# An FFT convolution with a gated GLU, forward and backward: four offset streams, two-bank PSUM tiles, and crossbar transposes moved into the GLU stage

## The chip, the core and the metric

One core of a Trainium2 chip runs the whole program. Its engines work side by side: PE (TensorE) multiplies matrices and writes only to PSUM; DVE (VectorE) and ACT (ScalarE) do elementwise work and carry PSUM to SBUF; POOL (GpSimd) and SP (SyncE) here mostly issue DMAs. The DMAs of all queues run on 16 DMA engines. The metric is the device time of one execution in microseconds, lower is better, as the median of several runs. A profile is one further execution, recorded by the hardware.

## The reference

The function has two halves that share a layer-normalized input, and the kernel returns its value and nine gradients:

```
def _A_ref(q, k, v, shift_k, ssm_k, ssm_D):       # S = 2048, D = 512, L = 2S
    k_shift = sum over t<4 of k_pad[:, t:t+S] * shift_k[:, 3-t]
    kv = k_shift * v
    y = irfft(rfft(kv_pad) * rfft(kf_pad))[:S]     # long convolution over S, per channel
    y = y + kv * ssm_D
    return q * y
def _B_ref(x, w_gate, w_up, w_down):               # F = 1376
    h = sigmoid(x @ w_gate) * (x @ w_up)
    return h @ w_down
xn = layernorm(A_q)
out = A_q + _A_ref(xn, A_k, A_v, ...) * silu(_B_ref(xn, ...))
# returned: out and the gradients of q, k, v, shift_k, ssm_k, ssm_D, w_gate, w_up, w_down for grad_out
```

All inputs and outputs are bf16.

## The kernel before, in words

Tokens lie so that token 16p + j is at partition p of block j: 16 blocks (NJ) of 128 tokens. The 512 channels are worked in four groups (NG) of 128 (GW). The 4096-point transform is a product of matrix steps on PE: `step1` multiplies by a cosine and sine table (Cf), `flip` transposes on PE, `step3` applies a small block-diagonal table (BD), `cmul` is the complex product on DVE (L411 to L415, four instructions), and `inv3`, `inv1` go back with R and Ci, the transposed table. Between steps each PSUM tile is carried to SBUF by `bal.evac` (L114), which gives the copy to ACT (it then shows as L121) or DVE (L124), whichever has the smaller sum of estimated work so far.

SBUF is one slab, from which an allocator hands out rings; a ring's tile can be written again when its last user is done. PSUM is one pool of eight banks of 2 KB: four one-bank tiles "mm", two "acc", two "tr".

The work is written as generators that yield after a piece of PE work. `run_streams` always advances the one with the smallest share of its total done, so the program's text order mixes them. The compiler of the kernel then orders each engine's instructions by that priority and by a timing model of its own, and sets the waits; on the chip each engine and each DMA queue runs its list in order.

Stage A (L545 to L549): `gluA` does the first LAG = 4 token blocks of the GLU's forward half (`f_gen`), `frontA` transposes ssm_k, forms k_shift and kv (`shift`: eight DVE instructions of 2048 elements in a row), and does step1 for both; `backA` does the rest and leaves y in y2A, and both spectra in the DRAM scratch KK_d.

Stage B (`stepB`, L677): 88 PE transposes of w_gate and w_up (`wT_prep`), then for each token block i: `z_gen` (h @ w_down, the gate, the output o0, dz), `d_gen` (dh, then dg and du), `f_gen(i+4)`, and `x_gen` (the gradient of x through the layer norm, o1). f_gen computes psG, its sigmoid on ACT, psU, and the product h on DVE. h, dg and du are feature-major (features on partitions); they are stored to the DRAM scratch hT_d, dgT_d, duT_d by the POOL queue.

Stage C (L886 to L890): `dW` forms the three weight gradients in nine jobs. Each job needs a token-major block L of h, dg or du of 2 MB; `ld_L` loads it with four crossbar transposes from DRAM on the SP queue (L743), two jobs ahead. `frontC` and `backC` do the backward FFT group by group: step1 on dy, flips, step3, two complex products with the spectra loaded by `ld_KK` (SP queue, L792), inverse steps, then the gradients of v, k, shift_k, ssm_k. A one-token shift inside SBUF (L842, 127 partitions) feeds the gradients of k and shift_k. Outputs go out on the POOL queue; dW's pass through a ring of three tiles (ot).

Of the kernel before, what the change touches and what calls it, by code (L numbers as in the profile page):

```python
# [8 lines left out]
ACT = mybir.ActivationFunctionType  # L9
# [20 lines left out]
LAG = 4  # L30
SLAB = 206 * 1024
# [95 lines left out]
def run_streams(streams, until=None):  # L127

    live = [[g, 0.0, float(tot)] for g, tot in streams]
    while live:  # L130
        if until is not None and until():
            return [(g, t - d) for g, d, t in live]
        order = sorted(live, key=lambda s: s[1] / s[2])
        for s in order:
            try:
                c = next(s[0])
            except StopIteration:
                live.remove(s)
                break
            if c:  # L140
                s[1] += c
                break
        else:
            raise RuntimeError("all streams blocked")
    return []
# [8 lines left out]
def gen_fft_consts(nc, ar, negpi, Cf, BD, R):  # L154
# [4 lines left out]
    def tmp(shape, dt):  # L159
# [8 lines left out]
    nc.vector.tensor_tensor(m, a[:, :, None].to_broadcast([P, 16, 128]),  # L168
                            b[:, None, :].to_broadcast([P, 16, 128]), ALU.mult)
    mc = tmp([2, 16, 128], i32)  # L170
    nc.vector.tensor_single_scalar(mc[:, 0], m, 6144, ALU.add)
    nc.vector.tensor_single_scalar(mc[:, 0], mc[:, 0], 8191, ALU.bitwise_and)
    nc.vector.tensor_single_scalar(mc[:, 1], m, 8191, ALU.bitwise_and)
    mf = tmp([2, 16, 128], f32)
    nc.vector.tensor_copy(mf, mc)
    nc.scalar.activation(Cf, mf, ACT.Sin, bias=negpi, scale=sc)
# [40 lines left out]
def kernel_impl(ctx, tc, A_q, A_k, A_v, A_shift_k, A_ssm_k, A_ssm_D, B_x, B_w_gate, B_w_up, B_w_down,  # L217
# [9 lines left out]
    hT_d = dram.tile([NJ * P, FP], bf16, name="hT_d")  # L227
    dgT_d = dram.tile([NJ * P, FP], bf16, name="dgT_d")
    duT_d = dram.tile([NJ * P, FP], bf16, name="duT_d")
# [4 lines left out]
    psp = ctx.enter_context(tc.tile_pool(name="ps", bufs=1, space=PSUM))  # L234
    bal = Bal(nc)

    def ps_mm(shape, dt=f32, name="ps_mm"):
        return psp.tile([P] + shape, dt, name=name, tag="mm", bufs=4)

    def ps_acc(shape, dt=f32, name="ps_acc"):  # L240
        return psp.tile([P] + shape, dt, name=name, tag="acc", bufs=2)

    def ps_tr(shape, dt=bf16, name="ps_tr"):
        return psp.tile([P] + shape, dt, name=name, tag="tr", bufs=2)

# [19 lines left out]

# [6 lines left out]
    make_identity(nc, ident)  # L272
    nc.vector.memset(neghalf, -0.5)
    T = [dict() for _ in range(NJ)]

# [17 lines left out]
    def f_gen(i):  # L293
# [4 lines left out]
        bal.evac(xnT, pt[:], 512, half=True)  # L298
# [5 lines left out]
        for pi, (f0, nb) in enumerate(FBS):  # L304
            psG = ps_mm([4, 128], name="psG")
            for b in range(nb):
                for db in range(4):
                    nc.tensor.matmul(psG[:, b, :], wg[:, db, (f0 + b) * 128:(f0 + b + 1) * 128], xnT[:, db, :],  # L308
                                     start=(db == 0), stop=(db == 3))
            nc.scalar.activation(sigT[:, f0:f0 + nb, :], psG[:, 0:nb, :], ACT.Sigmoid)  # L310
            bal.act(nb * 128)
            yield nb * 512
            psU = ps_mm([4, 128], name="psU")
            for b in range(nb):
                for db in range(4):
                    nc.tensor.matmul(psU[:, b, :], wu[:, db, (f0 + b) * 128:(f0 + b + 1) * 128], xnT[:, db, :],  # L316
                                     start=(db == 0), stop=(db == 3))
            nc.vector.tensor_tensor(hT[:, f0:f0 + nb, :], psU[:, 0:nb, :], sigT[:, f0:f0 + nb, :], ALU.mult)  # L318
# [3 lines left out]
            yield nb * 512  # L322
        nc.gpsimd.dma_start(hT_d[i * P:(i + 1) * P, :], hT.rearrange("p a t -> p (a t)"))


    f_x(0)
    f_x(1)
    nc.scalar.dma_start(wg[:, :, 0:F], B_w_gate.rearrange("(db p) f -> p db f", p=P))
    nc.sync.dma_start(wu[:, :, 0:F], B_w_up.rearrange("(db p) f -> p db f", p=P))
    nc.gpsimd.memset(wg[:, :, F:FP], 0.0)  # L330
    nc.gpsimd.memset(wu[:, :, F:FP], 0.0)
    with nc.allow_non_contiguous_dma(reason="tiny"):
        nc.gpsimd.dma_start(Dcol_b, A_ssm_D.rearrange("(cg p) -> p cg", p=P))
    f_ln(0)
    skr_r = Ring(ar, [D * 4])
    ones_r = Ring(ar, [P])
    skr, ones1 = skr_r.ap[0:1, :], ones_r.ap[0:1, :]
    nc.gpsimd.dma_start(skr, A_shift_k.rearrange("(o d) t -> o (d t)", o=1))
    nc.vector.memset(ones1, 1.0)
    gen_fft_consts(nc, ar, negpi, Cf, BD, R)  # L340
# [8 lines left out]
    Ci_r = Ring(ar, [2, 16, 128])  # L349
    Ci = Ci_r.ap  # L350
    KT_r = Ring(ar, [S])
    KC_r = Ring(ar, [NJ, GW])
    kh_r = Ring(ar, [NJ + 3, 2 * GW])
    vg_r = Ring(ar, [NJ, 2 * GW])
    acc_r = Ring(ar, [NJ, GW])
    term_r = Ring(ar, [NJ, GW])
    kvt_r = Ring(ar, [NJ, GW])
    QgK_r = Ring(ar, [2, GG, NJ, 8])
    QgV_r = Ring(ar, [2, GG, NJ, 8])
    Qf_r = Ring(ar, [2, GG, 128], n=1)  # L360
# [6 lines left out]
    flags = set()  # L367
    stA = {}

    def gen_ci():  # L370
        for c in range(2):
            for jh in range(2):
# [3 lines left out]
                bal.evac(Ci[:, c, 8 * jh:8 * jh + 8, :], pt[:], 1024, half=True)  # L376
                yield 1024

    def step1(src, Qg):
        for jb in range(4):  # L380
            for c in range(2):
                ps = ps_mm([4, GW], name="ps_q")
                for jj in range(4):
                    j = jb * 4 + jj
# [566 lines left out]
```

## Time and profile before

| what | value |
|---|---|
| runs of the kernel | 747.41, 748.88, 762.13 us; median 748.88 |
| profiled execution, its own time | 755.69 us |
| its span, first to last instruction | 753.9 us |
| mean granted TensorE clock | 0.919 |
| busy: PE, DVE, ACT, POOL | 586.7, 443.5, 371.6, 146.0 us |
| DMA | 94.83 MB in 113545 packets, 79926 of them under 512 B |
| stage A, to the first psZ matmul of stage B | 215.6 us |
| stage B, to the last psX matmul | 235.5 us |
| stage C | 302.8 us |

Busy time is the time in which an engine executes; its share of the span averages stages with different limits, so the stages are read apart. A row such as "L411 DVE TENSOR_TENSOR slab<-slab 128x1024 bf16 x48 | 33.1, 690 | 134.5 <-ACT slab L121 132.1" gives line, engine, operation, tiles and count; the busy time and the mean of one in ns; then the engine's idle time just before these instructions, and what ended it. "PEld" is the loading of weights into PE. The granted clock is the share of full speed that PE had. DMA share is the mean busy share of the 16 DMA engines.

### The profile page before, as it was taken

How to read it: one execution, taken by the hardware profiler on the slowest of the kernel's cores; microseconds unless marked ns; L12 is line 12 of the kernel's file. 1: busy time of each engine (PE TensorE's matmuls, PEld its weight loads, DVE VectorE, ACT ScalarE, POOL GpSimd, SP SyncE). 2: the span in 40 equal slices, each digit the busy share in tenths (PEclk: the TensorE clock that was granted, in tenths of full speed). 3: DMA queues.
4: the chain of work that ended last, by engine and by line, in shares of the span. 5: the costliest groups of instructions: out<-in, count | busy, mean ns of one | idle time of the engine just before them, and what ended most of it. 6: DMA issues, size and time to landing. Idle time of an engine off the chain costs nothing. (4 is left out here: it accounts for less than half of the span.)

```text
span 753.9 us, 13216 instructions
## 1 busy us (share of the span) xinstructions
PE 586.7 (78%) x5340; PEld 386.3 (51%) x5340; DVE 443.5 (59%) x904; ACT 371.6 (49%) x588; POOL 146.0 (19%) x224
## 2 busy tenths in 40 slices
PE   2277386788879999999999789599949944996650
PEld 1265174656647767776775444256425622554430
DVE  4399469583857877887787661027607520662643
ACT  3475285778744334433442222177517801782770
POOL 4012121120201111111111133000510230015011
PEclk9998598899999999999999899799979986998985
DMA  5425423134422232323229279669766699635106
GB/s 178 144 87 173 148 80 123 64 112 102 167 78 99 94 145 86 108 95 143 87 98 220 94 159 215 114 133 235 200 107 157 179 160 81 148 124 142 67 23 67
DMA packets 113545, 94.83 MB, mean 126 GB/s; under 512 B 79926, under 2 KB 97036, under 8 KB 113484
## 3 DMA queue, kind: packets, MB, share of 16 engines
q1 hardware_dynamic: 97580, 43.29, 26.5%
q0 software_dynamic: 15376, 49.30, 22.2%
q10 hardware_dynamic: 528, 1.41, 0.5%
q8 instruction: 41, 0.67, 0.4%
q14 instruction: 20, 0.16, 0.1%
HBM read 32.28 MB, written 42.51 MB: 99 GB/s over the span
## 5 line engine op out<-in xcount | busy, mean ns | idle before, releaser
L411 DVE TENSOR_TENSOR slab<-slab 128x1024 bf16<-128x1024 bf16 x48 | 33.1, 690 | 134.5 <-ACT slab L121 132.1
L772 PE MATMUL psW<-slab 128*128 128x512 bf16 (+1 forms) x384 | 86.2, 370 | 30.9 <-ACT slab L121 30.9
L427 PE MATMUL ps_b<-slab 128*128 128x256 bf16 x384 | 63.0, 298 | 34.7 <-DVE slab L414 33.8
L658 PE MATMUL psX<-slab 128*128 128x512 bf16 x352 | 82.5, 390 | 0.4 <-DVE slab L643 0.3
L121 ACT CAST slab<-ps_b 128x512 bf16<-128x512 f32 x96 | 52.4, 592 | 53.3 <-PE ps_b L427 51.7
L772 PEld LDWEIGHTS <-slab 128*128 128x128 bf16 x384 | 37.4, 99 | 64.9 <-issue 34.4
L427 PEld LDWEIGHTS <-slab 128*128 128x128 bf16 x384 | 33.9, 104 | 67.4 <-DVE slab L414 54.7
L121 ACT CAST slab<-ps_q 128x512 bf16<-128x512 f32 x82 | 47.2, 616 | 43.1 <-PE ps_q L385 30.8
L121 ACT CAST slab<-psW 128x512 bf16<-128x512 f32 (+1 forms) x35 | 20.0, 575 | 83.3 <-DMA out_dram<-slab 61.0
L658 PEld LDWEIGHTS <-slab 128*128 128x128 bf16 x352 | 34.2, 100 | 41.5 <-issue 2.9
L755 PE MATMUL psW<-slab 128*128 128x512 bf16 x176 | 44.0, 397 | 9.6 <-ACT slab L121 9.6
L308 PE MATMUL psG<-slab 128*128 128x128 bf16 x704 | 49.1, 224 | 0.6 <-DVE slab L318 0.4
L316 PE MATMUL psU<-slab 128*128 128x128 bf16 x704 | 48.8, 223 | 0.3
L639 PE MATMUL psD<-slab 128*128 128x128 bf16 x704 | 46.6, 220 | 1.2 <-ACT slab L121 1.2
L308 PEld LDWEIGHTS <-slab 128*128 128x128 bf16 x704 | 44.0, 101 | 3.2 <-issue 1.9
L385 PE MATMUL ps_q<-slab 128*128 128x128 bf16 x384 | 34.6, 228 | 14.1 <-ACT slab L121 11.4
L121 ACT CAST slab<-ps_x 128x512 bf16<-128x512 f32 x80 | 44.0, 626 | 1.5 <-PE ps_x L405 1.2
L639 PEld LDWEIGHTS <-slab 128*128 128x128 bf16 x704 | 42.2, 98 | 4.8 <-issue 1.2
L593 PE MATMUL psZ<-slab 128*128 128x512 bf16 x176 | 43.0, 393 | 1.0 <-DMA slab<-in_B_w_down_dram 1.0
L316 PEld LDWEIGHTS <-slab 128*128 128x128 bf16 x704 | 43.2, 100 | 0.9 <-issue 0.6
L121 ACT COPY slab<-ps_fl 128x1024 bf16<-128x1024 bf16 x39 | 37.5, 1041 | 11.9 <-PE ps_fl L395 11.7
L642 ACT CAST slab<-psD 128x512 bf16<-128x512 f32 (+1 forms) x48 | 26.0, 545 | 34.6 <-PE psD L639 33.4
(159 smaller groups left out, 1113.0 us busy)
## 6 DMA issues: line engine op xcount, KB each, us to landing
KK_d<-slab POOLq DMA_DIRECT2D x32, 256.0 KB, 3.1
slab<-KK_d SPq DMA_DIRECT2D x16, 512.0 KB, 4.1
out_dram<-slab POOLq DMA_DIRECT2D x58, 128.0 KB, 2.4
out_dram<-slab POOLq DMA_DIRECT2D x12, 512.0 KB, 7.3
hT_d<-slab POOLq DMA_DIRECT2D x16, 352.0 KB, 2.8
dgT_d<-slab POOLq DMA_DIRECT2D x16, 352.0 KB, 2.6
duT_d<-slab POOLq DMA_DIRECT2D x16, 352.0 KB, 3.6
slab<-in_A_q_dram SPq DMA_DIRECT2D x32, 128.0 KB, 2.4
```

Of the source, the lines that this page charges most:

```text
L121: self.nc.scalar.copy(dst, src)
L308: nc.tensor.matmul(psG[:, b, :], wg[:, db, (f0 + b) * 128:(f0 + b + 1) * 128], xnT[:, db, :], start=(db == 0), stop=(db == 3))
L316: nc.tensor.matmul(psU[:, b, :], wu[:, db, (f0 + b) * 128:(f0 + b + 1) * 128], xnT[:, db, :], start=(db == 0), stop=(db == 3))
L385: nc.tensor.matmul(ps[:, jj, :], Cf[:, c, j, :], src(j), start=True, stop=True)
L411: nc.vector.tensor_tensor(out=T1, in0=K, in1=X[:, 0:1, :].to_broadcast([P, 2, 512]), op=ALU.mult)
L427: nc.tensor.matmul(ps[:, gi].rearrange("p j x -> p (j x)"), Y[:, c, gg * 128:(gg + 1) * 128], R[:, c].rearrange("p j e c -> p (j e c)"), s ...
L593: nc.tensor.matmul(psZ[:], hT[:, fb, :], wd[:, fb, :], start=(fb == 0), stop=(fb == NFB - 1))
L639: nc.tensor.matmul(psD[:, b, :], wdT[:, db, (f0 + b) * 128:(f0 + b + 1) * 128], dzT[:, db, :], start=(db == 0), stop=(db == 3))
L642: nc.scalar.copy(dh[:, 0:nb, :], psD[:, 0:nb, :])
L658: nc.tensor.matmul(psX[:], srcT[:, fb, :], wT[:, fb, :], start=(n == 0), stop=(n == 2 * NFB - 1))
L755: nc.tensor.matmul(acc[:], L[:, b, j, :], dzA[:, j, :], start=(j == 0), stop=(j == NJ - 1))
L772: nc.tensor.matmul(acc[:, 0:nb, :], xnA[:, j, db * 128:(db + 1) * 128], L[:, 0:nb, j, :], start=(j == 0), stop=(j == NJ - 1))
```

## The change

The forward FFT becomes three streams: K (ssm_k: transposes, step1, flip), V (shift, step1, flip) and X (everything after the flips), beside G (f_gen). A stream now has a start and a rate, so that X begins at 0.2 of the others' progress, and K and V end at 0.8. The eight shift instructions are separate pieces. LAG goes from 4 to 3.

Every FFT step fills a PSUM tile of two banks and is evacuated 1024 wide. Stage A has three such tiles and two "tr"; stages B and C two such tiles, two "acc" and two "tr". f_gen puts G and U in the two banks of one tile; d_gen takes eight blocks and then three. bf16 evacuations of transposes are pinned to DVE, that of dz to ACT.

h, dg and du are turned token-major in stage B: a crossbar transpose from SBUF to SBUF on the SP queue, then a store on POOL into hS_d, dgS_d, duS_d, a little later in the program (`pend`). In stage C, `ld_L` is a plain load on SP, and `ld_KK` moves to POOL. w_gate and w_up are transposed by the crossbar on SP (most of it from DRAM) in place of PE. The weight gradients start as a second stream in the last tenth of B, with a job loaded ahead, and last to the end of C. Halo loads and the one-token shift are split at partition 112 or 113. The first loads of k, v and ssm_k go out at the start in memory of their own, and the table Cf is made in two halves without a conversion to f32. o2 and o3 are written, and v is read, two groups at a time.

```diff
-LAG = 4
-SLAB = 206 * 1024
+LAG = 3
+SLAB = 207 * 1024
...
 def run_streams(streams, until=None):
-    live = [[g, 0.0, float(tot)] for g, tot in streams]
+    live = [list(st) + [0.0] * (5 - len(st)) for st in streams]
...
+        for st in sorted(live, key=lambda s: s[2] + (s[3] - s[2]) * s[4] / s[1]):
...
+    def token_major(srcT, dst):
+        def store(st):
+            nc.gpsimd.dma_start(dst, st)
+
+        def tr():
+            st = stS_r[0].next()
+            nc.sync.dma_start_transpose(st.rearrange("p (a b) -> p a b", b=128), srcT.rearrange("p a t -> p (a t)"))
+            pend.insert(min(1, len(pend)), lambda: store(st))
+        pend.append(tr)
...
     f_gen
-            psG = ps_mm([4, 128], name="psG")
+            ps = ps_mm([2, 4, 128], name="psGU")
+            for k, w in ((0, wg), (1, wu)):
...
-        nc.gpsimd.dma_start(hT_d[i * P:(i + 1) * P, :], hT.rearrange("p a t -> p (a t)"))
+        token_major(hT, hS_d[i])
...
+    def ld_halo(eng, dst, src):
+        eng.dma_start(dst[1:113], src[0:112])
+        eng.dma_start(dst[113:128], src[112:127])
...
     step1 (flip, step3, inv3, inv1 and the dk step likewise)
-        for jb in range(4):
+        for jb in range(2):
             for c in range(2):
-                ps = ps_mm([4, GW], name="ps_q")
+                ps = ps_mm([8, GW], name="ps_q")
...
-    run_streams([(gluA(), LAG * 11776), (frontA(), 4 * 10240), (backA(), 4 * 36864 + 4096)])
+    run_streams([(strG(), LAG * 11776, 0.0, 1.0), (strK(), 4 * 10240, 0.0, 0.8), (strV(), 4 * 16384, 0.0, 0.8),
+                 (strX(), 4 * 28672 + 4096, 0.2, 1.0)])
...
+    PS["pool"], PS["mm"] = psB, 2
...
-    def wT_prep():
...
+    for w, src, dst in ((wg, B_w_gate, wgT), (wu, B_w_up, wuT)):
+        nc.sync.dma_start_transpose(dst[:, 0:NFB - 1, :], src[:, 0:128 * (NFB - 1)])
+        for db in range(4):
+            nc.sync.dma_start_transpose(dst[:, NFB - 1:NFB, db * 128:(db + 1) * 128], w[:, db, 128 * (NFB - 1):FP])
...
     d_gen
-        for f0, nb in FBS:
-            psD = ps_mm([4, 128], name="psD")
+        for f0, nb in ((0, 8), (8, 3)):
+            psD = ps_mm([8, 128], name="psD")
...
     ld_L
-            nc.sync.dma_start_transpose(L[:, 0:nb, 4 * q:4 * q + 4, :].rearrange("p f j t -> p f (j t)"),
-                                        srcs[s][q * 512:(q + 1) * 512, f0 * 128:(f0 + nb) * 128])
+            nc.sync.dma_start(L[:, 4 * q:4 * q + 4, 0:w], srcs[s][4 * q:4 * q + 4, :, f0:f0 + w].rearrange("j p f -> p j f"))
...
     ld_KK
-            nc.sync.dma_start(KK, KK_d[n // 4, n % 4].rearrange("t p c x -> p t c x"))
+            nc.gpsimd.dma_start(KK, KK_d[n // 4, n % 4].rearrange("t p c x -> p t c x"))
...
-            nc.sync.dma_start(dks[0:P - 1, NJ:NJ + 3, :], dks[1:P, 0:3, :])
+            nc.gpsimd.dma_start(dks[0:112, NJ:NJ + 3, :], dks[1:113, 0:3, :])
+            nc.gpsimd.dma_start(dks[112:127, NJ:NJ + 3, :], dks[113:128, 0:3, :])
...
-    run_streams([(frontC(), 4 * 4096), (backC(), 4 * 40960 + 4096), (dW(), 35 * 8192)])
+    live = run_streams([(gated(stepB(), "B"), 16 * 17920, 0.0, 1.0)], until=lambda: "fwd" in flags)
...
+    live = run_streams(live, until=lambda: "z15" in flags)
+    ot_r = Ring(ar, [512], n=3)
+    ld_L(0)
+    live = run_streams(live + [(dW(), 35 * 8192, 0.9, 1.8)], until=lambda: "B" in flags)
...
+    run_streams([(dw[0], dw[1] - dw[4], 0.0, 1.0), (frontC(), 4 * 4096, 0.0, 0.75), (backC(), 4 * 43008 + 4096, 0.03, 0.95)])
```

More of the change, by code (lines that the diff above doesn't have):

```diff
@@ L421, in inv3 @@
     def inv3(Y, qq, Bg):
[L422 to L431 removed]
+        ps = ps_mm([4, NJ, 16], name="ps_b")
@@ L502, in frontA @@
[L502 to L515 removed]
+            Qf = QfV_r.next()
+            yield from flip(Qg, Qf)
```

622 lines of the change are left out of this document (321 added, 301 removed).

## The prediction, made before the changed kernel was run

> **What bounds the kernel now.** I read the page first, then cut the trace into stages with the view of busy time by stretch, then asked for waits, and read order and rates from the timeline.
>
> ```profile
> PE 586.7 (78%) x5340; PEld 386.3 (51%) x5340; DVE 443.5 (59%) x904; ACT 371.6 (49%) x588; POOL 146.0 (19%) x224
> ```
> ```profile
> 0.00:38.00 38.00, 9.34 (x68) 7.08 (x69) 16.06 (x38) 14.18 (x15) 9.54 (x21) 1.00 0.50 162
> 38.00:215.60 177.60, 131.14 (x1384) 98.74 (x1384) 129.40 (x235) 118.06 (x198) 33.30 (x58) 0.89 0.36 119
> 215.60:451.10 235.50, 227.32 (x2400) 158.10 (x2400) 178.73 (x442) 91.30 (x159) 42.66 (x74) 0.97 0.37 114
> 451.10:753.90 302.80, 218.94 (x1489) 122.39 (x1487) 119.28 (x190) 148.08 (x216) 60.53 (x72) 0.88 0.67 135
> ...
> 240.00:400.00 160.00, 160.00 (x1865) 118.68 (x1862) 127.96 (x312) 67.33 (x118) 28.77 (x54) 1.00 0.30 107
> 500.00:540.00 40.00, 38.81 (x283) 21.95 (x281) 27.89 (x44) 32.11 (x46) 6.54 (x9) 1.00 0.75 185
> 600.00:640.00 40.00, 18.99 (x101) 9.42 (x98) 7.34 (x7) 6.25 (x13) 11.36 (x12) 0.74 1.07 126
> 696.00:753.90 57.90, 24.51 (x192) 15.51 (x192) 28.97 (x48) 28.81 (x40) 5.44 (x7) 0.77 0.29 51
> ```
>
> Columns: stretch, length, busy PE, PEld, DVE, ACT, POOL, then granted clock, DMA share, GB/s. Stage A (forward FFT, to 215.6) fills no engine: DVE is busiest, 73% after 38 us. Stage B (the GLU) is full: from 240 to 400 PE is busy all the time at clock 1.00 while the DMA engines are at 0.30. Stage C (weight gradients and backward FFT, 302.8 us) swings between 38.81 of 40 us on PE and 18.99 of 40, the latter where the DMA engines are full (1.07). It ends with 58 us in which PE is under half busy, since the weight gradients were used up.
>
> ```profile
> DVE slab L411 <- ACT slab L121: 132.1, 4, 45.7
> ACT slab L121 <- DMA out_dram<-slab: 61.0, 4, 23.2
> ```
> ```profile
> 467.78 1.89 PE L755 MATMUL psW<-slab 128*128 128x512 bf16 x8
> 479.31 3.57 PE L755 MATMUL psW<-slab 128*128 128x512 bf16 x8 [9.64 <-ACT slab L121]
> ...
> 478.68 0.59 ACT L121 CAST slab<-psW 128x512 bf16<-128x512 f32 x1 [13.79 <-DMA out_dram<-slab]
> ```
>
> The chain of a stall in C: an output store lands late, so the ring of three output tiles is full, so ACT cannot evacuate psW and all its queued evacuations stop, so PE and later DVE stop. The stores are late because the crossbar transposes of hT_d, dgT_d and duT_d fill the DMA engines.
>
> **The change, part by part.** Rates first.
>
> ```profile
> 455.89 3.62 PE L755 MATMUL psW<-slab 128*128 128x512 bf16 x16
> 459.56 4.48 PE L755 MATMUL psW<-slab 128*128 128x512 bf16 x20
> ...
> 396.23 0.83 PE L308 MATMUL psG<-slab 128*128 128x128 bf16 x12
> 227.92 1.06 PE L308 MATMUL psG<-slab 128*128 128x128 bf16 x16
> ...
> 215.64 6.56 PE L593 MATMUL psZ<-slab 128*128 128x512 bf16 x22 [0.99 <-DMA slab<-in_B_w_down_dram]
> 446.11 5.18 PE L658 MATMUL psX<-slab 128*128 128x512 bf16 x22
> ```
>
> Four more matmuls of 512 columns take 0.86 us, 0.215 each; of 128 columns 0.23, 0.057 each; 256 columns I take as half of 512, 0.108. One f_gen (92 narrow) is 5.2 us, a token block's d, z, x (48 narrow, 33 wide) 9.85, both 15.1.
>
> ```profile
> L411 DVE TENSOR_TENSOR slab<-slab 128x1024 bf16<-128x1024 bf16 x48 | 33.1, 690 | 134.5 <-ACT slab L121 132.1 <-DMA slab<-KK_d 0.5
> L414 DVE TENSOR_TENSOR slab<-slab 128x512 bf16<-128x512 bf16 x48 | 20.3, 423 | 2.5
> L469 DVE TENSOR_TENSOR slab<-slab 128x2048 bf16<-128x2048 bf16 x12 | 14.6, 1218 | 0.0
> L124 DVE COPY slab<-ps_fl 128x1024 bf16<-128x1024 bf16 x9 | 5.8, 686 | 2.6 <-PE ps_fl L395 2.6
> L318 DVE TENSOR_TENSOR slab<-psU,slab 128x512 bf16<-128x512 f32 x32 | 22.0, 689 | 8.0 <-PE psU L316 8.0
> L283 DVE BATCH_NORM_STATS2 slab<-slab 128x6 f32<-128x512 bf16 x16 | 10.9, 681 | 11.1 <-DMA slab<-in_A_q_dram 11.1
> ...
> L121 ACT CAST slab<-ps_q 128x512 bf16<-128x512 f32 x82 | 47.2, 616 | 43.1 <-PE ps_q L385 30.8 <-DVE slab L204 11.3 <-DVE slab L207 0.8
> L121 ACT COPY slab<-ps_fl 128x1024 bf16<-128x1024 bf16 x39 | 37.5, 1041 | 11.9 <-PE ps_fl L395 11.7
> L121 ACT CAST slab<-ps_dk 128x512 bf16<-128x512 f32 x16 | 36.1, 2677 | 0.0
> L310 ACT ACTIVATE slab<-psG 128x512 bf16<-128x512 f32 x32 | 19.1, 598 | 7.0 <-PE psG L308 6.3
> L288 ACT ACTIVATE slab<-slab 128x512 bf16<-128x512 bf16 x16 | 13.0, 832 | 9.0 <-DVE slab L287 9.0
> ```
>
> Stage A. The shift of k into the first products waits for a 127-partition halo load:
>
> ```profile
> 22.34 1.17 SPq L453 DMA_DIRECT2D slab<-in_A_k_dram  x1
> ...
> 37.48 1.23 DVE L466 TENSOR_TENSOR slab<-slab 128x2048 bf16<-128x2048 bf16 x1 [10.52 <-DMA slab<-in_A_k_dram]
> ...
> 725.39 0.62 SPq L842 DMA_DIRECT2D slab<-slab  x1
> ...
> 739.61 1.23 DVE L873 TENSOR_TENSOR slab<-slab 128x2048 bf16<-128x2048 bf16 x1 [9.11 <-DMA slab<-slab]
> ```
>
> By their shapes these are 190 KB in 15 us and, at the other end, 95 KB in 14 us, far below the 162 GB/s of the first 38 us. The change cuts them into 112 and 15 partitions and issues the k loads at once, in memory of their own. Ahead of the halo lie some 4.3 MB; 162 GB/s at share 0.50 makes 324 GB/s full, so 13 us at best and 27 at 162: the shift starts near 22, not 37.5. Then DVE has 16 complex products of 2.23 (two of 0.690, two of 0.423) = 36, 32 shift products of 1.22 = 39, 44 transpose evacuations pinned to it at 0.686 = 30, and some 11 for three f_gen (each three products at up to 0.689, statistics at 0.681 and small change): 116 us. ACT has 88 evacuations of 1024. The trace has none from f32; it lies between 1.04 (1024 wide from bf16) and 1.23 (twice 616), and I take 1.04, since the element count is the same: 92, plus 8 for three f_gen (each three sigmoids at up to 0.598 and a normalization at 0.832), so 100 against 118 now. At today's 73% DVE the rest takes 159 us, at 85% 136; with the shift products fed between other work instead of eight in a row I take 150. One f_gen leaves A. A ends at 22 + 150 = 172 (158 to 199; the latter is only the halo and f_gen gained).
>
> Stage B. PE then has 13 x 15.1 + 3 x 9.85 = 226 us, where it had 12 x 15.1 + 4 x 9.85 = 221 in 235.5: 15 us go to the pipeline's start and end. PE's 88 weight transposes go to the crossbar. On PE they are 88 x 0.057 = 5 us, mostly in A's gaps before B begins, so I count their going at nothing. On SP two loads of 1.3 MB, transposed, join that of w_down:
>
> ```profile
> 180.89 5.24 SPq L558 DMA_TRANSPOSE slab<-in_B_w_down_dram  x1
> ```
>
> Two more of 5 us, with eight small ones, lie under the last backward-FFT work of A, in memory that the K and V streams have left; uncovered they would cost up to 10 us, which the range holds. Three 352 KB SBUF-to-SBUF transposes an iteration are new, on SP, and a store of each behind it on POOL. The trace has transposes from DRAM of 512 KB or 384 KB:
>
> ```profile
> L743 SPq DMA_TRANSPOSE slab<-hT_d x12: 1557/3555/8016, 397.0 to 471.4; - x12
> L743 SPq DMA_TRANSPOSE slab<-dgT_d x12: 1445/2619/5167, 490.6 to 549.0; - x12
> L743 SPq DMA_TRANSPOSE slab<-duT_d x12: 1484/3278/12248, 571.0 to 644.2; - x12
> ```
>
> At their medians 352 KB is 2 to 2.5 us; the 95 KB SBUF shift on what looks like one engine gives 14 x 352/95/16 = 3.2 us over 16. So 6 to 10 us of a 15 us iteration, on DMA engines at 0.30: hidden, at about 0.8. Behind a waiting POOL store stand the power of the next layer norm and the output stores; the former is used an iteration later, so 5 us of wait is covered. Behind the transposes on SP stand loads issued two blocks ahead. If the cover goes, an iteration grows to what the transposes take (a rival below). A real cost is PSUM: four one-bank buffers become two of two banks. The first f_gen buffer after psD's eight blocks is psD's own, and PE must wait for ACT's 1024-wide copy (1.04 plus hand-over) unless the scheduler finds other matmuls: 0 to 1.3 us, I take 0.8, times 13 = 10. Weight-gradient matmuls enter at nine tenths of B: while B does its last tenth they advance by 0.1/0.9, so 0.11 x 112 us = 12, of which 6 fill B's end gaps. B is 226 + 15 + 10 + 12 - 6 = 257.
>
> Stage C. Matmuls: weight gradients 432 x 0.215 + 128 of 352 columns x 0.148 = 112; each of four backward groups 128 x 0.057 + 32 x 0.215 + 64 x 0.108 = 21.1; Ci 1.8: 198, less 12 done in B = 186. The transposes are gone; the loads left are plain. C's bytes by their shapes (15 MB of scratch, 8.4 of KK, 6.3 of v, k and ksh, 10.5 of outputs) are 40 MB and need 123 us at 324 GB/s, under 186, so output stores should land in time. What is late next: dk's strided evacuations, 5.4 us of ACT for each 1024 (twice 2.677), two in a row per group, while PE has diagonal matmuls (3.4) and two psW accumulators (6.9): 0 to 5 us, I take 3, times 4 = 12. KK loads queue behind output stores on POOL; they are due most of a quarter-group later (186/16, some 11 us), so I count them at nothing; if that cover goes, each of 16 could cost up to 5 us. Start of C 6, unfilled PE as in 500 to 540 (3%) 5, last evacuation and store 5; the 14 us shift and the 58 us tail go, since gradients now last to the end. C is 186 + 28 = 214, against 302.8.
>
> [...]
>
> **Sum.** 172 + 257 + 214 = 643, and 1.8 outside the span (755.69 less 753.9): 645 against 755.69. The profiled run lies 0.9% above the median of 748.88, so the forecast is 645 x 0.991 = 639 (620 to 660 on its own).
>
> **Rivals.** *A stays as loose as it is* (199): four streams still share two evacuating engines, whose work drops only by a tenth; 666. *The crossbar slows B*: at 4.5 us each with the engines near 1.0, loads and stores land late as they do in C now, and each of 16 iterations takes 3 us more; 684. *Better than taken*: A at 158, no PSUM wait, little dk wait; 607. *No change in C*: something other than transposes made stores late, so that PE still loses 100 us, and A's gain is lost in B; 745. Against it stand the good windows whose transposes were fewer.
>
> *Slower*: SBUF-to-SBUF transposes cost far more than those from DRAM. Three an iteration bind B above 5 us each; the gain of 110 us is gone at 5 + 110/48 = 7.3 us each. At the longest now seen (12.2) B is 16 x 36.7 = 587, the kernel 970. For it: no such transpose is in this trace. Against it: the medians and the shift's 3.2. [...]
>
> **Chances.** Forecast 0.60, loose A 0.14, slow crossbar 0.09, better 0.08, no change 0.04, slower 0.05. The range 600 to 700 takes in the first four with their spreads, some 0.83. 2% is about what the runs (747.41 to 762.13) can tell apart: faster 0.91, same 0.04, slower 0.05.
>
> **What would show it.** A: the first shift product near 22 us, B's first psZ matmul near 172. B: iterations of 15 to 16 us, SP transposes of 2 to 3 us, psGU waits on ACT of about 1 us. C: DMA share below 0.8, hardly a wait of ACT for output stores, PE over 85% busy to within 10 us of the end. Transposes above 5 us, or C's PE again at half, would make me wrong.

## The result, and the profile after

The changed kernel took 695.97 us (median of 4, 692.08 to 698.14), the kernel before, beside it, 752.76 (median of 4); the ratio is 0.9262 [0.9169, 0.9355]. The forecast was 639, with a range from 600 to 700: faster, as said, but by half as much (57 us in place of 110). Some executions ran in a slower state (672.0 us, beside 656.7, for the last kernel below); ratios and their 95% intervals leave them out and medians do not, so the two can differ by a per cent or two.

The page of the changed kernel, engine totals and two groups of its part 5:

```profile
PE 558.4 (80%) x5184; PEld 377.2 (54%) x5252; DVE 440.2 (63%) x888; ACT 321.9 (46%) x375; POOL 143.3 (21%) x242
...
L765 PE MATMUL psW<-slab 128*128 128x512 bf16 (+1 forms) x172 | 40.9, 391 | 17.8 <-DMA slab<-hS_d 14.7
...
L445 DVE TENSOR_TENSOR slab<-slab 128x1024 bf16<-128x1024 bf16 x48 | 33.1, 690 | 14.5 <-ACT slab L121 9.4
```

The wait that the prediction began with is gone: DVE's complex product waited 132.1 us for ACT, now 9.4, and no group shows ACT waiting for an output store. In its place PE waits 14.7 us for the first loads of h. Busy time by stretch (columns as in the prediction):

```profile
201.07:382.56 181.49, 171.27 (x1932) 124.72 (x1954) 134.72 (x314) 64.08 (x103) 30.46 (x56) 1.00 0.68 168
...
440.50:660.20 219.70, 193.71 (x1386) 115.94 (x1408) 120.09 (x197) 116.80 (x110) 53.83 (x84) 0.95 0.55 164
440.50:460.00 19.50, 4.70 (x29) 2.41 (x30) 3.01 (x7) 2.74 (x3) 5.14 (x8) 0.70 1.07 214
...
660.00:680.00 20.00, 0.16 (x1) 0.00 (x0) 11.09 (x15) 4.28 (x1) 4.40 (x5) 0.59 0.89 97
675.00:680.00 5.00, 0.00 (x0) 0.00 (x0) 0.00 (x0) 0.00 (x0) 0.00 (x0) 0.50 1.14 20
```

In the middle of stage B PE is busy 94%, where it was full; some two matmuls of each block are missing from this trace (it has 162 of 176 for psZ), and the trace of the first experiment below, whose stage B is the same, has them and shows 96% (174.41 of 181.49 us). Stage C starts with 19.5 us in which PE works 4.7, and ends with 36 us (660.2 to 696.4) in which it does nothing; at 675 the DMA engines are busy (1.14) and move 20 GB/s. Rows of the timeline (start, duration, engine, instruction, idle time before it and its releaser):

```profile
19.09 1.22 DVE L508 TENSOR_TENSOR slab<-slab 128x2048 bf16<-128x2048 bf16 x1
...
241.94 2.54 PE L615 MATMUL psZ<-slab 128*128 128x512 bf16 x10
257.90 2.54 PE L615 MATMUL psZ<-slab 128*128 128x512 bf16 x10
...
323.75 2.54 PE L615 MATMUL psZ<-slab 128*128 128x512 bf16 x10
...
436.68 6.58 SPq L285 DMA_TRANSPOSE slab<-slab  x2
443.35 0.56 SPq L749 DMA_DIRECT2D slab<-hS_d  x1
458.01 1.89 PE L765 MATMUL psW<-slab 128*128 128x512 bf16 x4 [12.52 <-DMA slab<-hS_d]
...
666.21 0.90 POOL L895 DMA_DIRECT2D out_dram<-slab  x1
666.99 0.85 POOL L894 DMA_DIRECT2D out_dram<-slab  x1
670.04 1.22 DVE L886 TENSOR_TENSOR slab<-slab 128x2048 bf16<-128x2048 bf16 x1
671.56 1.12 POOL L890 DMA_DIRECT2D out_dram<-slab  x1 [3.71 <-DVE slab L886]
```

A token block now takes 15.96 us (241.94 to 257.90; before, 15.1). The last piece of job 1 of dW is issued at 443.35, behind two transposes on SP, and PE gets it at 458. At the end POOL issues out_6 (L895, single values of 2 bytes), out_4 (L894, runs of 8 bytes) and then the last 1 MB of o2, 25 us before the span's end.

The stages, against the forecast:

| stage | before | forecast | measured |
|---|---|---|---|
| A, to the first psZ matmul | 215.6 | 172 | 173.5 |
| B, to the end of the last psX matmul | 235.5 | 257 | 267 |
| C | 302.8 | 214 | 256 |

### The profile page after: what moved, and what is told of

Read it like the earlier page. It is cut to its first block, busy times and chain, and to the rows that moved or that the text cites. A ratio compares the mean times of both kernels' runs of the same rounds, so it can differ in the third digit from the quotient of the medians.

```text
span 696.4 us, 12768 instructions
## 1 busy us (share of the span) xinstructions
PE 558.4 (80%) x5184; PEld 377.2 (54%) x5252; DVE 440.2 (63%) x888; ACT 321.9 (46%) x375; POOL 143.3 (21%) x242
## 2 busy tenths in 40 slices
DMA packets 140962, 114.51 MB, mean 164 GB/s; under 512 B 91190, under 2 KB 126472, under 8 KB 140904
## 5 line engine op out<-in xcount | busy, mean ns | idle before, releaser
L322 PE MATMUL psGU<-slab 128*128 128x128 bf16 x1408 | 90.1, 223 | 9.0 <-DVE slab L325 4.7
L322 PEld LDWEIGHTS <-slab 128*128 128x128 bf16 x1408 | 85.1, 100 | 15.7 <-issue 13.7
L768 PE MATMUL psW<-slab 128*128 128x512 bf16 (+1 forms) x371 | 84.6, 356 | 1.1 <-ACT slab L121 0.5
L121 ACT CAST slab<-ps_b 128x1024 bf16<-128x1024 f32 x48 | 49.0, 1023 | 37.8 <-PE ps_b L459 37.6
L324 ACT ACTIVATE slab<-psGU 128x512 bf16<-128x512 f32 (+1 forms) x48 | 27.1, 564 | 69.3 <-PE psGU L322 69.2
L121 ACT CAST slab<-ps_x 128x1024 bf16<-128x1024 f32 x48 | 48.4, 1031 | 22.3 <-PE ps_x L439 21.5
L124 DVE COPY slab<-ps_fl 128x1024 bf16<-128x1024 bf16 x48 | 32.1, 687 | 40.3 <-PE ps_fl L428 40.0
L688 ACT ACTIVATE slab<-slab 128x512 f32<-128x512 f32 x16 | 13.1, 816 | 95.4 <-DVE slab L687 95.4
L121 ACT CAST slab<-ps_q 128x1024 bf16<-128x1024 f32 x48 | 48.6, 1044 | 15.4 <-PE ps_q L418 15.4
L765 PE MATMUL psW<-slab 128*128 128x512 bf16 (+1 forms) x172 | 40.9, 391 | 17.8 <-DMA slab<-hS_d 14.7
L121 ACT CAST slab<-psW 128x512 bf16<-128x512 f32 (+2 forms) x35 | 20.3, 579 | 60.5 <-PE psW L765 40.9
L445 DVE TENSOR_TENSOR slab<-slab 128x1024 bf16<-128x1024 bf16 x48 | 33.1, 690 | 14.5 <-ACT slab L121 9.4
L765 PEld LDWEIGHTS <-slab 128*128 128x128 bf16 (+1 forms) x176 | 17.9, 103 | 39.2 <-DMA slab<-hS_d 15.4
```

Of the source, the lines that this page charges most:

```text
L121: self.nc.scalar.copy(dst, src)
L124: self.nc.vector.tensor_copy(dst, src)
L322: nc.tensor.matmul(ps[:, k, b, :], w[:, db, (f0 + b) * 128:(f0 + b + 1) * 128], xnT[:, db, :], start=(db == 0), stop=(db == 3))
L324: nc.scalar.activation(sigT[:, f0:f0 + nb, :], ps[:, 0, 0:nb, :], ACT.Sigmoid)
L445: nc.vector.tensor_tensor(out=T1, in0=K, in1=X[:, 0:1, :].to_broadcast([P, 2, 512]), op=ALU.mult)
L765: nc.tensor.matmul(acc[0:kf, :], L[:, j, b * 128:b * 128 + kf], dzA[:, j, :], start=(j == 0), stop=(j == NJ - 1))
```

## The experiments

Times are medians of four executions; a ratio is to the kernel before run beside it (medians from 751 to 758 us), and kernels are compared by their ratios first. Intervals in brackets that overlap leave a difference open.

**The end of the kernel: paired stores, or small pieces?** First o2 and o3 stored for each group (o2 is shown):

```diff
-            if cg % 2 == 1:
-                nc.gpsimd.dma_start(o2C[:, :, c0 - GW:c1], stC["dk"])
+            nc.gpsimd.dma_start(o2C[:, :, c0:c1], dk)
```

> The changed kernel, with o2 and o3 stored for each group of 128 channels (512 KB each) and no longer for two groups at once. In the changed kernel TensorE's last matmul ends at 660.2 us, VectorE's last product at 671.3, the 1 MB store of o2 is issued at 671.6 and the span ends at 696.4. Theory P (pairing: what is stored last is twice as large): half of o2 and o3 leaves a group earlier, the last store lands some 7 us after its issue as a 512 KB store did in the kernel before, and the time falls by 12 to 18 us. Theory S (the small scattered stores of out_4 and out_6, issued at 667.0 and 666.2 ahead of o2 on the same queue, hold o2 up): the stores' number stays, so 0 to 5 us less.

693.49 us, ratio 0.9264 [0.9191, 0.9337]: no change. Theory P falls.

Then the small stores on another queue:

```diff
-            nc.gpsimd.dma_start(out_4..., skout)        # and out_6
+            nc.sync.dma_start(out_4..., skout)
```

> The changed kernel, with the two small stores at the end (out_4 in runs of 8 bytes, out_6 in single values of 2 bytes) issued on SP's queue in place of POOL's, so that they no longer lie ahead of o2 there. Theory S (small stores hold o2 up in the queue): o2 moves its 1 MB in some 8 to 10 us at the 114 to 256 GB/s of the stretches around it, the end is then set by o2 or by the small stores (some 10 to 15 us by themselves), and the time falls by 10 to 16 us. Theory P (pairing): o2 is as large as before, so 0 to 3 us less. A third possibility, that the small writes are slow on the engines whichever queue brings them: they still land 24 us after their issue near 667, so 5 us less at most.

684.86, ratio 0.9123 [0.9056, 0.9190], 1.4 points lower and as theory S had it, though the intervals just overlap: from the last VectorE product to the end 15 us, not 25. But the small stores themselves still took 15.7 us (out_6) and 18.5 (out_4) to land. So the number of pieces was changed: a product with a column of ones gathers a group's 512 values of out_4 on one partition, and another turns the column of out_6 into a row. These rows go out on SP's queue, group by group.

```diff
-            nc.vector.tensor_reduce(res[:, cg, :], dm, AX.X, ALU.add)
+            nc.tensor.matmul(prow, onec, dm, start=True, stop=True)     # 1 x 512
+            nc.sync.dma_start(out_4[c0:c1, :], row)                     # one piece of 1 KB
```

> The changed kernel with only out_4 and out_6 written as rows, as in the run beside it (o2 and o3 still for two groups at once, all on POOL's queue as changed). Theory S (number of small pieces): the 25 us from the last VectorE product to the end become 8 to 12, so 13 to 17 us less than 695.97: 679 to 683, and less than with the small stores moved to SP (684.86). Theory P (pairing): 0 to 4 us less.

683.03, ratio 0.9016 [0.8941, 0.9091], 13 us less by the medians and 18 by its profile (span 678.7). Its timeline, and below it DMA issues with the median from issue to landing, of the changed kernel and of this one:

```profile
669.57 1.23 DVE L894 TENSOR_TENSOR slab<-slab 128x2048 bf16<-128x2048 bf16 x1
671.09 1.12 POOL L898 DMA_DIRECT2D out_dram<-slab  x1 [6.23 <-DVE slab L894]
```
```profile
out_dram<-slab POOLq DMA_DIRECT2D x4, 1024.0 KB, 15.7
...
out_dram<-slab POOLq DMA_DIRECT2D x1, 1.0 KB, 24.8
out_dram<-slab POOLq DMA_DIRECT2D x1, 4.0 KB, 24.2
```
```profile
out_dram<-slab POOLq DMA_DIRECT2D x4, 1024.0 KB, 7.1
```

These rows are medians of four stores of 1 MB. The last of the four, o2, issued at the same place, took 23.0 us to land before and 6.0 with the rows, and the end comes 8 us after the last product in place of 25: 5 KB in 1024 pieces had cost 17 us. In the kernel before they had been issued 21 and 5 us ahead of the last store.

Which of the two small stores is dear was not tried apart, but the DMA packets kept with the trace of the kernel before point to out_6. Its 512 pieces of 2 bytes, 16 packets of 64 bytes in the trace, went out at 729.6 to 731.4 us, the pieces of 8 bytes of out_4, 16 packets of 256, at 744.0 to 744.3. Of the 256 packets of 4,096 bytes that started between the two, 33 took 1.5 to 5.0 us, where the median is 0.2; of the 128 after out_4, none did. The stretch of the changed kernel with 1.14 of the engines busy at 20 GB/s agrees that something there is dear, but no run here shows why.

**The start of stage C: order of the jobs.** Job 2 is loaded early, into the buffer that job 0 leaves; job 1's buffer is memory that B frees last.

```diff
-        for n, (s, c) in enumerate(jobs):
+        for n in (0, 2, 1, 4, 3, 6, 5, 8, 7):
+            s, c = jobs[n]
```

> The changed kernel, with the weight-gradient jobs worked off in the order 0, 2, 1, 4, 3, 6, 5, 8, 7. Job 2 (352 columns of h) is loaded from 417 us on into the buffer that job 0 leaves; job 1 waits for memory that the GLU stage frees only at its end, and its last piece lands at 458. Theory W (the wait at the start of the last stage, 12.5 + 2.2 us of TensorE, is paid in full): job 2's 48 matmuls of 512 columns (48 x 0.215 = 10 us) fill it, and the time falls by 9 to 13 us. Rival D (that stretch is bound by transfers, at a DMA share of 1.07): what TensorE gains there it waits for later, at job 1 or at the first KK, and 0 to 4 us are left.

686.66, ratio 0.9145 [0.9071, 0.9220]: 9 us less by the medians, as theory W had it, with intervals that overlap. PE's waits for loads of h in this kernel, from the view of waits (us in total, times, longest):

```profile
PE psW L766 <- DMA slab<-hS_d: 4.0, 1, 4.0
```

**What did the split of the halo transfers do?** One part of the change alone, put into the kernel before:

```diff
-        nc.sync.dma_start(kh[1:, 0:3, :], kHalo[:, 0:3, c0:c1])
+        nc.sync.dma_start(kh[1:113, 0:3, :], kHalo[0:112, 0:3, c0:c1])
+        nc.sync.dma_start(kh[113:128, 0:3, :], kHalo[112:127, 0:3, c0:c1])
```

and likewise L809 and L842.

> The kernel before, with one part of the change alone: the halo loads of k and the shift of dks within SBUF are cut into 112 and 15 partitions. Theory N (a transfer over 127 partitions runs on one engine or few, some 14 us for 95 to 190 KB): each takes 2 to 5 us, the first shift product starts near 27 us in place of 37.5, and the last one's wait of 9.1 us near the end is gone; in all 12 to 22 us less than the kernel before. Rival (latency and waiting in the queue, not the number of partitions): the pieces take as long, and the time stays within 4 us.

701.20, ratio 0.9357 [0.9277, 0.9437]: 50 us, more than theory N had, though the first shift product came at 30.6 us and not at 27. The transfers of three lines, cut in two, give 6.4% where the whole change gives 7.4%. The timelines of POOL, the kernel before and then this one, show where:

```profile
608.94 4.46 POOL L809 DMA_DIRECT2D slab<-in_A_k_dram  x1
613.31 1.74 POOL L778 DMA_DIRECT2D out_dram<-slab  x3
632.57 1.07 POOL L778 DMA_DIRECT2D out_dram<-slab  x2 [17.52 <-ACT slab L121]
```
```profile
566.79 0.81 POOL L810 DMA_DIRECT2D slab<-in_A_k_dram  x1
567.50 0.68 POOL L811 DMA_DIRECT2D slab<-in_A_k_dram  x1
568.10 1.74 POOL L779 DMA_DIRECT2D out_dram<-slab  x3
580.84 1.07 POOL L779 DMA_DIRECT2D out_dram<-slab  x2 [11.01 <-ACT slab L121]
```

Before, each group's backward FFT loads the halo of k on POOL's queue (at 447.5, 542.4, 608.9 and 681.4 us); three output stores of dW go out behind it (after the first load only at 466.9, behind other transfers), and the next one only 10 to 19 us after them, since the ring of three output tiles is full. PE stalls once after each load: 9.64, 9.88, 21.01 and 6.38 us (those over 3 us). With the split one of 8.78 is left. The shifts of L842, split in the same run, are issued at 526.9, 592.2, 669.6 and 725.4 us and lie in none of these stalls. Landing times of that load, before and split:

```profile
slab<-in_A_k_dram POOLq DMA_DIRECT2D x4, 95.2 KB, 13.8
```
```profile
slab<-in_A_k_dram POOLq DMA_DIRECT2D x4, 84.0 KB, 6.0
```

The packets of the traces show how the load differs. The one at 608.94 is 23 packets of 4,096 bytes and one of 3,328, one behind another from 618.6 to 626.9 us. With the split, 112 partitions are 16 packets of 4,096 and 16 of 1,280 bytes; in the changed kernel, which has the same split, those of the load at 464.21 start side by side, all 32 between 465.66 and 466.22 us. Whether the stores wait for the long load in their queue or at the DMA engines, no run tells apart: the eight transposes on SP's queue beside the third load took longer as well, 45.5 us against 34.8 with the split.

Next, the prediction's own cause taken away instead: plain loads in place of the transposes, in the kernel before.

```diff
-            nc.sync.dma_start_transpose(L[...], srcs[s][rows, cols])
+            nc.sync.dma_start(L[...], srcs[s][rows, cols])      # same bytes, not transposed
```

> The kernel before, with the 36 crossbar transposes of the last stage replaced by plain loads of as many bytes into the same buffers (the weight gradients are then taken from blocks that were not transposed; the work on the engines is the same). Halo loads and shifts stay in one transfer of 127 partitions. Theory H: the stalls stay where they are, behind the halo loads; what goes is at most the wait of 21 us at 632, which had eight slow transposes beside it, so 5 to 25 us less than the kernel before. Theory X, that of the prediction: with the transposes gone the stores land in time and the stalls of 9.6, 9.9 and 21 us and the tail they leave go, 60 to 100 us less.

732.98, ratio 0.9830 [0.9731, 0.9929]: theory H's range; theory X falls. The four stalls of PE are still there, at 3.68, 10.33, 9.57 and 6.36 us; the first and the third are shorter. Both taken away:

> The kernel before with both causes of the late stores taken away: halo loads and shifts in 112 and 15 partitions, and plain loads in place of the transposes in the last stage (the weight gradients are again taken from blocks that were not transposed). Split alone took it from 750.8 to 701.2, plain loads alone from 751.2 to 733.0. If the stalls need both (a long transfer on the queue, and engines full beside it), one removal leaves little for the other: 692 to 700. If they are separate costs that add up: 680 to 686.

688.57, ratio 0.9251 [0.9163, 0.9340]: between the two expectations. The waits decide better than the times. The group of ACT's psW evacuations (idle time before them, then its causes) with the split, with plain loads, and with both:

```profile
L121 ACT CAST slab<-psW 128x512 bf16<-128x512 f32 (+1 forms) x35 | 20.1, 577 | 49.6 <-DMA out_dram<-slab 27.0 <-PE psW L773 15.2 <-PE psW L756 7.0
```
```profile
L121 ACT CAST slab<-psW 128x512 bf16<-128x512 f32 (+1 forms) x35 | 20.1, 576 | 68.4 <-DMA out_dram<-slab 44.0 <-PE psW L772 16.1 <-PE psW L755 7.8
```
```profile
L121 ACT CAST slab<-psW 128x512 bf16<-128x512 f32 (+1 forms) x35 | 20.0, 575 | 37.9 <-PE psW L773 14.2 <-DMA out_dram<-slab 12.0 <-PE psW L756 8.2
```

ACT waited 61.0 us for stores before; 27.0 with the split, 44.0 with plain loads, 12.0 with both. The parts add up: 34 us go with the halo transfers, 17 with the transposes, and some 12 are left without either; their cause stays open.

The reverse, the changed kernel with only the split undone:

> The changed kernel with only the split undone: the halo loads of k and the shift of dks move 127 partitions in one transfer each, as before the change. Theory H (the split is what the change is worth, because a 127-partition transfer on POOL's queue holds up the output stores behind it, as after 447, 542, 609 and 681 us in the kernel before): the stalls come back, 20 to 50 us more than the changed kernel, so 715 to 746. Rival X (the stores were late because of the crossbar transposes, which have left the last stage): the long transfers are now mostly covered, 0 to 12 us more.

703.57, ratio 0.9412 [0.9327, 0.9497], 1.5 points above the changed kernel, with intervals that overlap: the range of X, a miss for H. Stage A ends 9 us later (182.7), and stage C is no longer than in the changed kernel (251.6 us, 256). ACT's wait for stores comes back, but smaller, and after the stage's start no stall of PE is longer than 3.4 us:

```profile
ACT slab L121 <- DMA out_dram<-slab: 18.8, 5, 7.4
```

So the same long transfers cost ACT less here: 18.8 us of waiting for stores, 61.0 in the kernel before and 44.0 there with plain loads. What stands behind them differs: in the kernel before three stores of dW in a row; the changed kernel spreads them, one or two at a time. Which part of the change spares the stalls here was not tried apart.

**What do the crossbar transposes cost in stage B?**

```diff
-            nc.sync.dma_start_transpose(st..., srcT...)
-            pend.insert(min(1, len(pend)), lambda: store(st))
+            pend.insert(min(1, len(pend)), lambda: store(srcT))
```

> The changed kernel without the 48 SBUF-to-SBUF crossbar transposes of the GLU stage: the blocks of h, dg and du are stored as they are (the weight gradients are then taken from blocks that were not transposed; bytes stored and loaded, and the work on TensorE, VectorE and ScalarE, are the same). Theory F of the prediction (they are hidden beside TensorE): 0 to 5 us less than the changed kernel's 695.97, iterations of the GLU stage stay at 16.5 us, and TensorE keeps its 6% of idle time there. Rival (they make the iteration 16.5 in place of 15.3 us, since VectorE or the stores wait for their buffers): 13 iterations of 1.2 us, so 12 to 20 us less, and TensorE is full in that stage.

673.58, ratio 0.9059 [0.9007, 0.9110]: 22 us by the medians, 15 by the ratios, the rival's size but not its place. Timeline of this kernel:

```profile
240.03 2.54 PE L613 MATMUL psZ<-slab 128*128 128x512 bf16 x10
255.98 2.54 PE L613 MATMUL psZ<-slab 128*128 128x512 bf16 x10
...
319.79 2.54 PE L613 MATMUL psZ<-slab 128*128 128x512 bf16 x10
...
433.37 11.36 PE L763 MATMUL psW<-slab 128*128 128x512 bf16 x43 [2.03 <-DMA slab<-hS_d]
```

A block still takes 15.95 us, and PE is hardly fuller (173.57 of 181.9 us; in the changed kernel 171.27 of 181.49). Five blocks took 16.36 each in the changed kernel (241.94 to 323.75), 15.95 here (240.03 to 319.79). That is one long block, and it is not shown to come from the transposes: in the first experiment, with the same stage B, five blocks took 15.95 as well (241.87 to 321.60). From the first psX matmul to the last B is 8 us shorter (243.8, was 252.2), most of it at the stage's end: from the psZ matmul at 371.62 to the end of B it was 69 us, here from 367.64 63. The wait at the start of C is 2.0 in place of 14.7 us: together 21. The DMA engines, at 0.68 in the middle of B, are at 0.30 without the transposes. What each transpose took in the changed kernel (min, median, max ns on SP's queue; us to landing):

```profile
L285 SPq DMA_TRANSPOSE slab<-slab x48: 1367/1558/4335, 165.7 to 441.3; - x48
...
DMA to landing us min/median/max: 3.5/4.3/14.5
```

**The PSUM of stage B**, as before the change:

```diff
-            ps = ps_mm([2, 4, 128], name="psGU")
+            pss = [ps_mm([4, 128], name="psGU") for _ in range(2)]    # one bank each, four buffers
-        for f0, nb in ((0, 8), (8, 3)):
+        for f0, nb in FBS:                                            # 4, 4, 3 blocks of psD
```

> The changed kernel with the PSUM of the GLU stage as before the change: four buffers of one bank (G and U apart, D in pieces of 4, 4 and 3 blocks with three ScalarE copies) in place of two of two banks. The prediction put 0.8 us per iteration on this, 10 us in all. If the 5 to 6% of TensorE's idle time in that stage is this: TensorE is full from 201 to 381 us (20 of 20, as in the kernel before), iterations fall from 16.5 to about 15.3, and the time by 10 to 18 us. If the idle time has another cause (the order in which the streams are interleaved, or records that are missing), 0 to 4 us less.

689.37, ratio 0.9094 [0.9001, 0.9187], with an interval that just overlaps the changed kernel's; the profiled span fell by 8 us, between the two expectations. Its timeline:

```profile
272.68 2.54 PE L620 MATMUL psZ<-slab 128*128 128x512 bf16 x11
287.79 2.54 PE L620 MATMUL psZ<-slab 128*128 128x512 bf16 x11
300.93 3.20 PE L682 MATMUL psX<-slab 128*128 128x512 bf16 x14 [1.50 <-DVE slab L669]
```

Undisturbed blocks are back at 15.1 us; others wait up to 1.7 us for the products dg and du, a wait that the run without transposes did not have there. So the two-bank tiles cost 0.85 us in an undisturbed block, and less on the mean: eleven blocks took 15.6 us each (194.75 to 366.76), in the changed kernel 16.1 (194.72 to 371.62). Stage B as a whole is 257.6 us, was 267. Why some blocks now wait for dg and du stays open.

**Put together.** Small stores on SP and the new order of jobs:

> The changed kernel with two of the single edits together: the two small stores on SP's queue, and the weight-gradient jobs in the order 0, 2, 1, 4, 3, 6, 5, 8, 7. Alone they took 695.97 to 684.86 and 686.66. If they act at two places (the end, the start of the last stage), the gains of 11 and 9 add up: 674 to 679. If the gain at the start is only moved to the end, 681 to 686.

676.30, ratio 0.9048 [0.8959, 0.9136]: 20 us less by the medians, 16 by the ratio, so by and large they add up. With the gradients spread further (`1.0` to `1.12` in the last `run_streams`):

> As the run with both edits, and the stream of weight gradients in the last stage is spread to 1.12 of the stage in place of 1.0, so that the backward FFT of the last group is done earlier and its VectorE products (19 us after the last TensorE matmul now) and stores lie beside matmuls that are left. If the end is set by the chain from the last group's inverse FFT through VectorE to the stores: 8 to 15 us less than the run with both edits, 662 to 670. If TensorE's sum of work sets it (the evacuation and store of the last weight gradient follow instead), 0 to 5 us less.

671.06, ratio 0.8976 [0.8887, 0.9065]; in the profiles the last product ended at 659, not 657, and the span was 671.6, not 672.4. No effect is shown. Then the small stores for each group in the middle of the stage:

> As the last run (weight-gradient order 0, 2, 1, ..., spread to 1.12), with the small stores issued on SP's queue for each group as soon as it has them, so that only a quarter of them (128 runs of 8 bytes and 128 of 2 bytes) is left at the end, and with o2 and o3 stored for each group. That run took 671.06; its last VectorE product ended at 659 us and its span at 671.6. If the small writes (15.7 and 18.5 us to land on SP's queue) and the 1 MB store still set the end together, a quarter and a half of them leave some 5 to 6 us after the last product: 663 to 667. If what is left is a fixed latency: 668 to 672.

688.83, ratio 0.9253 [0.9164, 0.9342]: a clear miss, and slower. ACT's waits for output stores, in the run before this one and in this one:

```profile
ACT slab L121 <- DMA out_dram<-slab: 16.3, 2, 11.0
```
```profile
ACT slab L121 <- DMA out_dram<-slab: 34.9, 5, 14.9
```

The 512 KB stores now take 12.1 us to land; with o2 and o3 stored for each group alone, in the first experiment, they took 5.4, and the time had not changed. The four stores of 1 KB of out_4 took 24.6 us to land (median), so the small pieces look as dear in the middle as at the end, and there more stores stand beside them; the two edits were not run apart in this order of jobs. With rows in their place:

> The run with order 0, 2, 1, ... and spread 1.12 (671.06), with out_4 and out_6 written as rows: a product with a column of ones gathers a group's 512 values of out_4 on one partition (1 KB in one piece), another transposes the group's column of out_6 (256 bytes in one piece), so that 8 stores of one piece each take the place of 1024 pieces of 8 and 2 bytes. If the number of small pieces is what slows o2 at the end (12.3 us from its issue to the span's end in that run), 4 to 8 us less: 663 to 667. If o2's own 1 MB sets it, 668 to 672; the row products cost TensorE and VectorE some 1 us per group.

669.16, ratio 0.8818 [0.8738, 0.8899]: faster than both kernels. Against the run with small pieces on SP at the end (671.06) it is 2 us by the medians, which is the rival's range, and 1.6 points by ratios whose intervals just overlap. From o2's issue to the end it is 7.8 us in place of 12.3. With the one-bank PSUM as well:

> The run with rows, order 0, 2, 1, ... and spread 1.12 (669.16; 0.8818 of the kernel before), and the PSUM of the GLU stage in four buffers of one bank (alone: 695.97 to 689.37, iterations of 15.8 in place of 16.4 us between 240 and 320 us). If the stage is bound by TensorE and its PSUM, the gain of about 0.6 us an iteration stays: 6 to 9 us less, 660 to 664, ratio 0.870 to 0.875. If the last stage then only waits for the last pieces of h, dg and du, 0 to 3 us less.

661.37 (656.7 to 672.0), ratio 0.8825 [0.8704, 0.8947]: by its time in the first expectation, by its ratio in the second. It cannot be told from the run above it, so it stays open whether that gain holds.

## Why the prediction was half right

The measured 696 us lies outside the forecast's own 620 to 660. It lies inside 600 to 700 because that range takes in the rivals, and neither rival that reaches so far is what happened: A did not stay loose, and slow transposes did not make output stores late. That is luck. The span was forecast at 643 and measured at 696.4; of the 53 us, stage A has 1.5, B 10 and C 42.

**A: right.** First shift product "near 22", measured 19.09; end at 172 (22 + 150), measured 173.5 (19.1 + 154.4), so the start was 3 us better than forecast and the rest 4 worse. With the split alone in the kernel before, A ended at 200.8: about 15 of its 42 us are the halo, 27 the rest.

**B: 10 us short (257, measured 267).** The PSUM term had the right size (10 us; with one-bank tiles B is 9 us shorter) but not the wait it named, PE waiting for ACT's copy of psD. PE's waits in the changed kernel from 201 to 383 us are for VectorE: for the product h, which frees the tile of G and U, and for dz.

```profile
PE psGU L322 <- DVE slab L325: 4.0, 12, 0.5
PE ps_dzT L645 <- DVE slab L626: 3.2, 11, 0.3
```

"Hidden, at about 0.8" failed for the transposes: with DMA share at 0.68 and SP's queue shared, they cost 8 us here, and 13 more where the prediction did not look, at the start of C. The price of one was forecast at 2 to 3 us, 1.6 on the queue was measured; the slower rival, with 7.3 us each, was far off.

**C: the step that failed (214, measured 256).** Its terms: matmuls 186, PE was busy 193.7; "start of C 6", idle before 460 was 14.8 (19.5 less 4.7); dk and unfilled PE 17, the rest of the idle time to 660.2 is 11.2 (219.7 - 193.7 - 14.8); "last evacuation and store 5", measured 36.2. So +8, +9, -6 and +31 make the 42. The largest miss is the last term: the prediction shows no row for its 5 us. In the kernel before it is about right, 6 us from the issue of the last store (747.71) to the end of the span, since both small stores had landed by then; the change puts them 5 us ahead of o2, still in flight. Eleven of the 36 are VectorE's last products, which run beyond PE's end; 25 are the stores, of which the rows took away 17. The trace of before had a sign of it, which the prediction read past; in its list of DMA issues the 1 KB of out_6 takes twice the 7.3 us (median) of a 512 KB store to land, and the 4 KB of out_4 half of it:

```profile
out_dram<-slab POOLq DMA_DIRECT2D x1, 1.0 KB, 14.5
out_dram<-slab POOLq DMA_DIRECT2D x1, 4.0 KB, 3.5
```

**The cause of the stalls was in the main wrong.** "The stores are late because the crossbar transposes ... fill the DMA engines": of ACT's 61 us of waiting 17 went with the transposes, 34 with the split of the halo transfers. The prediction had read from the trace that the transfers over 127 partitions were slow (95 KB in 14 us), and priced it at two places where an engine visibly waited for it (the first and the last shift). At L809 nobody waits for the load itself; the waiting is done by the stores behind it, and is booked to them. The total for C did not suffer from this, since the change removes both causes.

What the parts of the change are worth cannot be divided. The split alone gives 6.4%, all the rest without the split 5.9% (0.9412), both 7.4%: either way most of the stalls go. Against the kernel with the split alone, stage A is 27 us shorter, C 5 shorter (261 to 256), and B 36 longer (231 to 267): 19 us of work moved into it (one f_gen, 14 us of weight gradients), and the 8 and 9 us above.

The change also divides the DMAs anew between the queues of SP and POOL. No run undid that alone, so its worth stays open. One run bears on it: moving the two small stores to SP's queue took 1.4 points (10 us) off, where issuing them had taken POOL 1.8 us; on SP they also went out 4 to 10 us earlier (656.5 and 662.8 us, in place of 666.2 and 667.0). So there the queue was worth more than issue time, as far as the overlapping intervals let it be said.

## What to carry to other kernels

When a store lands late, look at what was issued ahead of it, on its own queue first, also at transfers for which nobody waits: here a load that took 13.8 us to land stood ahead, and the stall was booked to the stores behind it. Look at the number and the size of a transfer's pieces, not only at its bytes (here 5 KB in 1024 pieces cost 17 us), and see what a stage's last instructions leave in flight. "Hidden" work in a full stage, on a queue whose order others depend on, still had a price here, 8 us in the stage and 13 after it; most of it turned up at the stage's end and where the next stage starts.

## What was not expected of the hardware

A load of 95 KB over 127 partitions took POOL 4.4 us to issue and 13.8 to land; cut at 112 it took 0.8 + 0.7 to issue and the larger part landed in 6.0; the store after the three behind it came 10 to 19 us later, with the split 5 to 13. Its 97,536 bytes went one packet behind another, 24 of them in 8.3 us for the third such load. Stores of 1 KB and 4 KB in pieces of 2 and 8 bytes took 24 to 25 us when issued one right behind the other, and the 1 MB behind them 23.0 in place of 6.0; in the kernel before, apart, they took 14.5 (2 bytes) and 3.5 (8 bytes). The 48 transposes inside SBUF come as some 69,000 of the 140,962 packets (71,842 without them), 1,440 for each 352 KB.
